# Top-32 thresholds from all 576 columns instead of folded maxima and minima, with the first attention steps ahead of the weights in the planner's order

## The chip, the cores and the metric

One core of one Trainium2 chip. The metric is the device time of one execution in microseconds (us), lower is better. Five engines work from their own instruction queues and wait for each other through semaphores: PE (TensorE, the matmuls), DVE (VectorE), ACT (ScalarE), POOL (GpSimd) and SP (SyncE, which here issues all the DMAs). Each engine takes its own instructions strictly in the order of the program.

## The reference

Sparse attention, and then two feed-forward blocks, over 4 batches of 8 heads and 576 positions of 64 (2304 tokens of 512):

```python
scores = (1 / sqrt(64)) * q @ k.T                       # [4, 8, 576, 576]
kth = np.partition(scores, -32, axis=-1)[..., -32:-31]  # the 32nd largest of each row
scores = np.where(scores >= kth, scores, -1e9)
attn = softmax(scores); x = attn @ v                    # then tokens x 512
h = x @ w_in;  g = np.maximum(0.01 * h, h);  x = g @ w_out            # 512 -> 2048 -> 512
h = np.maximum(np.maximum(x @ w1, x @ w2), x @ w3);  out = h @ w_out2 # 512 -> 768 -> 512
```

## The kernel before

**The work.** Attention is cut into 72 steps. A step takes 128 rows of queries for two heads (for the last 64 rows of a batch, four heads), and there are 18 steps to a batch. The 2304 tokens go through the feed-forward blocks in ten units of 192, 128, 256 (six times), 192 and 256 tokens. A unit has four phases on PE: H (times `w_in`), Y (times `w_out`), M (times `w1`, `w2`, `w3`) and O (times the last weight). A unit can begin when the attention steps of its tokens are done, and it is spread between later steps. Values are kept as two fp16 halves, so each product is three matmuls (`three`, lines 824 to 827).

**One step.** PE computes the scores into PSUM (L689), ACT copies them to the tile `S` (L694). DVE finds the 32nd largest score of each row: L697 folds the row of 576 into 288 maxima and 288 minima of pairs (two instructions, tile `w`), L705 (MAX8: the eight largest of a row) and L707 (MATCH_REPLACE8: overwrite these eight, with a short MATCH_VALUE_LOAD ahead of it) take turns on maxima and minima, and L711 and L715 merge the two lists. For both heads (index `j`) together that is 2 folds, 12 MAX8, 8 MATCH_REPLACE8 and the two small merges. POOL derives the softmax bias from the row's maximum (L728, tile `nb`), ACT takes the exponential (L738, tile `pp`), DVE masks (L743 for the first head, mask and product in one; L747 for the second, whose product L750 is POOL's), ACT and POOL split into halves (L752, L754, tile `phl`), a transposing DMA (L757) brings the tile `pt`, PE multiplies by V (L782 to L784, tile `av`), DVE takes the reciprocal of the row sum (L789, L791), and the block's result goes through a second transposing DMA (L819) to the tile `xu`, from which H starts.

**Weights.** They arrive as 64-bit floats. DVE rebuilds fp32 words from them (three instructions each: L479, L482, L485, 42 groups), then come norms and scales, and ACT and POOL split them into halves (L348 to L350). The 42 groups are 8 of `w_in`, 8 of `w_out`, 18 of `w1` to `w3` and 8 of the last weight. The M phase ends each tile on DVE with L966 (`k<-h,colt,k`), 12 to a unit.

**Order.** Nothing above is in program order by hand. Each instruction is first a node with an engine, an estimated duration and a priority `pr` (lower goes first); `Plan.run` plays the nodes through the five engines with these durations and writes the program in the order that comes out. So the constants `mm`, `act`, `dve`, `pool`, `dma`, the latencies and the priorities decide only the order. `TP(i)` is the priority of step `i`: 0 for the first `NE` steps and 10 + 11.9 i from then on. Weights have `wt`, which starts at 2 and grows by 1.5 to 2.1 per chunk, with extra gaps `WGT` and `WGZ` ahead of `w1` and of the last weight.

Of the kernel before, what the change touches and what calls it, by code (L numbers as in the profile page):

```python
# [12 lines left out]
I32 = mybir.dt.int32  # L13
# [6 lines left out]
HP = H // 2  # L20
# [25 lines left out]
MMO = 1.0  # L46
# [6 lines left out]
NE = 2  # L53
TE = 0.0

# [146 lines left out]
def act(n, psum=False, aps=0):  # L202
    return (n * 0.833 + (53 if psum else 93) + 93 * aps) / 1000
# [6 lines left out]
def pool(n):  # L210
    return (n * 2.08 + 60) / 1000


def dma(nbytes):
    return nbytes / 360e3
# [3 lines left out]
def attention_moe_kernel(ctx, tc, qk, v, w_in, w_out, w123, w2o, outT):  # L219
# [85 lines left out]
    def total(cols, r, pr):  # L305

        p = buf("h", [P, 512])

        def mms():
            for i, c in enumerate(cols):  # L310
                T.matmul(p()[:, :c.shape[1]], ones32, c, start=i == 0, stop=i == len(cols) - 1,
                         skip_group_check=True)

        op(PE, 0.5 * len(cols), mms, r=r, w=[p], pr=pr)
        return p

    def pow2(key, n2, n, r, pr, pre=2.0, s=None, b=None):
# [3 lines left out]
        if pre == 2.0:  # L321
            op(DVE, 0.1, lambda: V.tensor_scalar(t, (n2() if callable(n2) else n2).bitcast(I32), 24, None,
# [6 lines left out]
        op(POOL, 0.17, lambda: G.tensor_scalar(s, t, -8388608.0, 204 * 8388608.0, op0=ALU.mult, op1=ALU.add),  # L329
           r=[(key, "t")], w=[(key, "s")], pr=pr)  # L330
        op(POOL, 0.17, lambda: G.tensor_scalar(b, t, 8388608.0, 50 * 8388608.0, op0=ALU.mult, op1=ALU.add),
# [23 lines left out]
    def prep_qk(b, hp, pr, fast):  # L355
# [4 lines left out]
        for a in (1, 0):  # L360
# [20 lines left out]
        op(POOL, 0.16, lambda: G.tensor_tensor(es, bi[:, 0:1], bi[:, 1:2], op=ALU.mult),  # L381
           r=[(("qk", b, hp, a), "b") for a in range(2)], w=[(kb, 0)], pr=pr)
        op(POOL, 0.17, lambda: G.tensor_scalar(es2[:, 0:1], es, 0.125, None, op0=ALU.mult),
           r=[(kb, 0)], w=[(kb, 1)], pr=pr)
        op(POOL, 0.17, lambda: G.tensor_scalar(es2[:, 1:2], es, -0.125, None, op0=ALU.mult),
# [4 lines left out]

    DQK = {}
# [40 lines left out]
    def prep_v(b, hp, pr):  # L432
# [15 lines left out]
        op(POOL, 0.2, ones_, w=[(t, 2)], pr=pr)  # L448
# [131 lines left out]
    def fin_in(pr):  # L580
# [5 lines left out]
        op(POOL, 0.18, lambda: G.tensor_scalar(e, bin_, kap, 2.0 ** -15, op0=ALU.mult, op1=ALU.mult),  # L586
# [3 lines left out]
    def fin_out(pr):  # L590
# [14 lines left out]
        op(POOL, 0.16, lambda: G.tensor_tensor(k2, SC["kap"], SC["kap"], op=ALU.mult), r=[("kap", "s")], w=["k2"],  # L605
           pr=pr)
        op(POOL, 0.18, lambda: G.tensor_scalar(c1_, k2, s1, FCI * 2.0 ** -30, op0=ALU.mult, op1=ALU.mult),
           r=["k2", "s1"], w=["cc1"], pr=pr)
        op(POOL, 0.16, lambda: G.tensor_tensor(c2, c1_, m1, op=ALU.mult), r=["cc1", "m1"], w=["ccy"], pr=pr)
        SC["cy"] = c2  # L610

    def fin_1(pr):
# [4 lines left out]
        op(POOL, 0.18, lambda: G.tensor_scalar(e, bt, kap, 2.0 ** -15, op0=ALU.mult, op1=ALU.mult),  # L617
           r=[("kap2", "s")] + [(("w", "t", c), "b") for c in range(NF2)], w=["e_1"], pr=pr)
        op(POOL, 0.16, lambda: G.tensor_tensor(c0, ikap, SC["ikap"], op=ALU.mult),
# [3 lines left out]
    def fin_2(pr):  # L623
        b2 = col(4)
        op(POOL, 0.18, lambda: G.tensor_scalar(b2, bz, SC["c0"], 2.0 ** 30, op0=ALU.mult, op1=ALU.mult),
# [30 lines left out]
    def TP(i):  # L656
        return TE if i < NE else TA0 + TA * i

# [5 lines left out]
    def fused(i, j):  # L664
        return j < FM

    def attention(i):
# [28 lines left out]
        for x, o in ((0, ALU.max), (1, ALU.min)):  # L696
            op(DVE, dve(S), lambda x=x, o=o: V.tensor_tensor(wp()[:, :, x], Sp()[:, :, :S2], Sp()[:, :, S2:], op=o),  # L697
               r=[(Sp, 0), (Sp, 1)], w=[(wp, 0, x), (wp, 1, x)], pr=pd)
        for x, g in [(0, 0), (0, 1), (1, 0), (0, 2), (1, 1), (0, 3), (1, 2), (0, 4), (0, 5), (0, 6)]:
            for j in range(2):  # L700
                r, c0 = g // 2, TOPK * x + 8 * (g // 2)
                mc = lambda j=j, c0=c0: m()[:, j, c0:c0 + 8]
                wx = lambda j=j, x=x: wp()[:, j, x]
                if g % 2 == 0:
                    op(DVE, dve(S2), lambda mc=mc, wx=wx: V.max(mc(), wx()), r=[(wp, j, x)], w=[(m, j, x, r)], pr=pd)  # L705
                else:
                    op(DVE, dve(S2), lambda mc=mc, wx=wx: V.match_replace(  # L707
                        out=wx(), in_to_replace=mc(), in_values=wx(), imm_value=NEG),
                       r=[(m, j, x, r)], w=[(wp, j, x)], pr=pd)
        KM = TOPK // 2  # L710
        op(DVE, 0.11, lambda: V.tensor_tensor(m()[:, :, TOPK:TOPK + KM], m()[:, :, TOPK:TOPK + KM],  # L711
                                              m()[:, :, TOPK - 2:TOPK - 2 - KM:-1], op=ALU.min),
           r=[(m, j, 0, r) for j in range(2) for r in range(1, 4)], w=[(m, j, 1, r) for j in range(2) for r in range(2)],
           pr=pd)
        op(DVE, 0.11, lambda: V.tensor_reduce(m()[:, :, TOPK + KM], m()[:, :, TOPK - 1:TOPK + KM], axis=AX.X,  # L715
                                              op=ALU.max),
           r=[(m, j, 0, 3) for j in range(2)] + [(m, j, 1, r) for j in range(2) for r in range(2)],
           w=[(m, j, 2) for j in range(2)], pr=pd)
# [7 lines left out]
        if full:  # L726
            e2 = ES[b, hps[0]]
            op(POOL, 0.245, lambda: G.tensor_scalar(nb(), m()[:, :, 0:1].rearrange("p a o -> p (a o)"), e2[:, 1:2],  # L728
                                                  LNPS, op0=ALU.mult, op1=ALU.add),
# [296 lines left out]
    for hp in range(2):  # L1026
        prep_batch(0, hp)
# [111 lines left out]
```

## Time and profile before

| | |
|---|---|
| time, median of 3 runs (lowest, highest) | 1182.51 us (1181.02, 1184.38) |
| the profiled execution: its own time, its span | 1183.1 us, 1181.3 us |
| PE busy | 926.9 us (78%) |
| DVE busy | 999.3 us (85%) |
| ACT busy | 760.8 us (64%) |
| POOL busy | 755.0 us (64%) |

The span runs from the first to the last instruction of the program; the time has 1.8 us more around it. Busy time is an average over stages: attention fills the span up to 1061 us, and feed-forward work alone fills the rest.

### The profile page before, as it was taken

The numbers are of one execution on the slowest core, as the hardware profiler recorded it, in microseconds if no ns is written. First come the engines' busy times: TensorE is split into PE (matmuls) and PEld (weight loads), VectorE is DVE, ScalarE is ACT, GpSimd is POOL, SyncE is SP. The second block draws the span as 40 slices with busy tenths as digits, with TensorE's granted clock in tenths as the row PEclk, the third lists the DMA queues.
The fourth block names the chain that finished last, engine by engine and source line by source line (L and its number), as shares of the span: only waits on it lengthen the run. The fifth ranks groups of instructions, "written<-read, shape, count | busy, mean of one in ns | idle before, by whom it ended". The sixth has DMA issues, their size and how long they took to land.

```text
span 1181.3 us, 28138 instructions
## 1 busy us (share of the span) xinstructions
PE 926.9 (78%) x10294; PEld 807.8 (68%) x10294; DVE 999.3 (85%) x2970; ACT 760.8 (64%) x1625; POOL 755.0 (64%) x1054
## 2 busy tenths in 40 slices
PE   3123333568898699899899978999998998999998
PEld 2112222467788588788778867878877887799987
DVE  4869999999999989999999999999969999991001
ACT  6665766667768678666668767676676566474331
POOL 5697776677668676656767676676775566473231
PEclk9999985569899799999999999999999999999999
DMA  7786156533654635354564336525553342331000
GB/s 248 251 254 193 43 145 180 167 103 90 140 96 106 123 93 127 73 99 68 109 145 114 79 71 135 100 51 125 120 124 73 77 74 58 57 89 27 14 1 19
DMA packets 268555, 125.84 MB, mean 107 GB/s; under 512 B 237440, under 2 KB 255360, under 8 KB 266368
## 3 DMA queue, kind: packets, MB, share of 16 engines
q1 hardware_dynamic: 268416, 124.04, 44.1%
q8 instruction: 81, 1.33, 0.5%
q14 instruction: 58, 0.48, 0.1%
HBM read 62.65 MB, written 14.16 MB: 65 GB/s over the span
## 4 chain that ended last, share of the span: by engine, by line
DVE 42%; PE 22%; POOL 15%; DMA 10%; issue 6%; ACT 4%; SPq 0%; POOLq 0%; ACTq 0%; DVEq 0%
DVE m L705 14%; DVE w L707 11%; DMA pt<-phl 8%; DVE w L697 4%; PE h L826 4%; PE h L825 4%; PE h L827 4%; POOL phl L754 3%; DVE pp L743 3%; PE acc L826 2%; PE acc L827 2%; PE acc L825 2%; POOL pp L750 2%; DVE S L747 2%; PE s L689 2%
## 5 line engine op out<-in xcount | busy, mean ns | idle before, releaser
L705 DVE MAX8 m<-w 128x8 f32<-128x288 f32 x864 | 343.5, 442 | 0.0
L882 POOL TENSOR_TENSOR f16t<-k,f16t 128x256 f16<-128x256 f32 (+2 forms) x220 | 152.2, 693 | 177.7 <-ACT f16t L876 169.2
L707 DVE MATCH_REPLACE8 w<-m,w 128x288 f32<-128x288 f32 x576 | 249.3, 439 | 0.0
L754 POOL TENSOR_TENSOR phl<-pp,phl 128x576 f16<-128x576 f32 x144 | 187.4, 1310 | 32.3 <-ACT phl L752 30.3
L825 PE MATMUL h<-k,w 128*128 128x256 f16 (+2 forms) x720 | 190.2, 268 | 15.7 <-ACT k L962 9.2
L826 PE MATMUL h<-k,w 128*128 128x256 f16 (+2 forms) x720 | 190.5, 268 | 9.0 <-POOL k L924 9.0
L827 PE MATMUL h<-k,w 128*128 128x256 f16 (+2 forms) x720 | 190.6, 269 | 0.0
L826 PE MATMUL acc<-f16t,wo 128*128 128x256 f16 (+2 forms) x640 | 166.2, 264 | 8.8 <-POOL f16t L882 8.6
L825 PE MATMUL acc<-f16t,wo 128*128 128x256 f16 (+2 forms) x640 | 166.4, 264 | 0.4 <-ACT k L919 0.4
L827 PE MATMUL acc<-f16t,wo 128*128 128x256 f16 (+2 forms) x640 | 166.4, 264 | 0.0
L825 PE MATMUL h<-xu,wi 128*128 128x256 f16 (+1 forms) x576 | 156.8, 272 | 6.9 <-ACT k L869 4.6
L826 PE MATMUL h<-xu,wi 128*128 128x256 f16 (+1 forms) x576 | 156.8, 272 | 0.0
L827 PE MATMUL h<-xu,wi 128*128 128x256 f16 (+1 forms) x576 | 156.7, 272 | 0.0
L752 ACT ACTIVATE phl<-pp 128x576 f16<-128x576 f32 x144 | 97.3, 681 | 81.6 <-DVE pp L743 37.6
L750 POOL TENSOR_TENSOR pp<-pp,S 128x576 f32<-128x576 f32 x72 | 98.3, 1366 | 73.2 <-DVE S L747 53.1
L689 PE MATMUL s<-kt,qt 128*128 128x288 f16 (+5 forms) x800 | 108.5, 287 | 38.8 <-ACT S L694 37.1
L738 ACT ACTIVATE pp<-S,nb,colt 128x576 f32<-128x576 f32 x144 | 120.4, 860 | 27.7 <-POOL nb L728 17.6
L697 DVE TENSOR_TENSOR w<-S 128x576 f32<-128x576 f32 x144 | 131.0, 912 | 5.3 <-ACT S L694 5.3
L876 ACT ACTIVATE f16t<-k 128x256 f16<-128x256 f32 (+2 forms) x220 | 86.0, 391 | 61.4 <-DVE k L966 58.7
L826 PEld LDWEIGHTS <-w 128*128 128x128 f16 x960 | 95.5, 100 | 28.5 <-issue 19.7
L782 PE MATMUL av<-vt,pt 128*128 128x65 f16 (+1 forms) x800 | 90.9, 202 | 30.2 <-DMA pt<-phl 26.7
L827 PEld LDWEIGHTS <-w 128*128 128x128 f16 x960 | 95.7, 100 | 22.6 <-issue 13.9
(136 smaller groups left out, 2585.7 us busy)
## 6 DMA issues: line engine op xcount, KB each, us to landing
w<-in_w SPq DMA_DIRECT2D x18, 512.0 KB, 4.2
w<-in_w_in SPq DMA_DIRECT2D x8, 1024.0 KB, 6.0
w<-in_w_out SPq DMA_DIRECT2D x8, 1024.0 KB, 5.0
raw<-in_qk SPq DMA_DIRECT2D x24, 288.0 KB, 3.3
dqk<-hl SPq DMA_DIRECT2D x48, 144.0 KB, 2.5
kt<-dqk SPq DMA_DIRECT2D x16, 288.0 KB, 3.2
qt<-dqk SPq DMA_DIRECT2D x144, 32.0 KB, 2.3
raw<-in_v SPq DMA_DIRECT2D x12, 352.0 KB, 3.3
```

What stands on the lines that cost most here:

```text
L689: T.matmul(p()[osl, h, o:o + w], q()[:, hh, st, :n], k()[:, hh, kc:kc + w], start=st == 0, stop=st == 1, skip_group_check=True)
L697: op(DVE, dve(S), lambda x=x, o=o: V.tensor_tensor(wp()[:, :, x], Sp()[:, :, :S2], Sp()[:, :, S2:], op=o), r=[(Sp, 0), (Sp, 1)], w=[(wp, 0 ...
L705: op(DVE, dve(S2), lambda mc=mc, wx=wx: V.max(mc(), wx()), r=[(wp, j, x)], w=[(m, j, x, r)], pr=pd)
L707: op(DVE, dve(S2), lambda mc=mc, wx=wx: V.match_replace(out=wx(), in_to_replace=mc(), in_values=wx(), imm_value=NEG), r=[(m, j, x, r)], w= ...
L738: op(ACT, act(S, aps=2), lambda j=j, es=es: A.activation(pp()[:, j], Sb[j](), AF.Exp, bias=nb()[:, j:j + 1], scale=es[:, 0:1]), r=[(Sp, j) ...
L750: op(POOL, pool(S), lambda j=j: G.tensor_tensor(p2(j), p2(j), mk(j), op=ALU.mult), r=[(Sp, j)], w=[(pp, j)], pr=pr)
L752: op(ACT, act(S), lambda j=j: A.activation(phl()[:, 0, j], pp()[:, j], AF.Copy), r=[(pp, j)], w=[(phl, 0, j)], pr=pr)
L754: op(POOL, pool(S), lambda j=j: G.tensor_tensor(phl()[:, 1, j], pp()[:, j], phl()[:, 0, j], op=ALU.subtract), r=[(pp, j), (phl, 0, j)], w= ...
L825: T.matmul(out, wt(0), xt(0), start=first, stop=False, skip_group_check=True)
L826: T.matmul(out, wt(0), xt(1), start=False, stop=False, skip_group_check=True)
L827: T.matmul(out, wt(1), xt(0), start=False, stop=last, skip_group_check=True)
L882: op(POOL, pool(N) + 0.044, lambda: G.tensor_tensor(hl()[:, 1, :N], g()[:, 0, :N], hl()[:, 0, :N], op=ALU.subtract), r=[(g, 0), (hl, 0)], ...
```

## The change

The fold is left out. Each head's row of 576 scores is searched directly: four MAX8 and three MATCH_REPLACE8 over 576 columns per head, 8 and 6 per step, the first pair reading `S` itself. The threshold is the eighth value of the fourth list, so the merges are gone too. The old search stays in the code behind `fold(i)`, which gives "N" (the new search) for every step.

The planner's numbers change as well. The first four steps (`NE`) get priorities 0, 2, 4, 6 and so stand ahead of nearly all weights; the queries and keys of all four head pairs of batch 0 are prepared at the start (`range(HP)`), without the wait `GQ` for an earlier write; the gaps `WGT` and `WGZ` go to 0. Most duration estimates are raised. The planner now also lets the first unit's H phase wait for all of `w_out`, its M phase for all of `w1` to `w3` and of the last weight, and the second unit's H phase for the last weight. No instruction outside the search is added or removed.

```diff
-MMO = 1.0
+MMO = 3.0
-NE = 2
+NE = 4
 TE = 0.0
+TS = 2.0
...
-    return (n * 0.833 + (53 if psum else 93) + 93 * aps) / 1000
+    return (n * 0.833 + (70 if psum else 120) + 105 * aps) / 1000
...
-    return (n * 2.08 + 60) / 1000
+    return (n * 2.13 + 110) / 1000
...
-    return nbytes / 360e3
+    return nbytes / 255e3
...
-               r=z0 + ([("d", 0, 0, 0, 1)] if b == 0 and hp > 1 else []), pr=pr,
+               r=z0 + (GQ if b == 0 and hp > 1 else []), pr=pr,
...
+    GQ = []
...
     def TP(i):
-        return TE if i < NE else TA0 + TA * i
+        return TE + TS * i if i < NE else TA0 + TA * i
...
-        for x, o in ((0, ALU.max), (1, ALU.min)):
-            op(DVE, dve(S), lambda x=x, o=o: V.tensor_tensor(wp()[:, :, x], Sp()[:, :, :S2], Sp()[:, :, S2:], op=o),
...
+        if md == "N":
+            thr = lambda j: m()[:, j, TOPK - 1:TOPK]
+            tk = lambda j: [(m, j, 0, 3)]
+            wj = lambda j: wp()[:, j].rearrange("p x s -> p (x s)")
+            for g in range(7):
+                for j in range(2):
+                    r = g // 2
+                    mc = lambda j=j, r=r: m()[:, j, 8 * r:8 * r + 8]
+                    src = (lambda j=j: Sb[j]()) if g < 2 else (lambda j=j: wj(j))
+                    rd = [(Sp, j)] if g < 2 else [(wp, j, 0)]
+                    if g % 2 == 0:
+                        op(DVE, dve(S) * 1.03, lambda mc=mc, src=src: V.max(mc(), src()), r=rd, w=[(m, j, 0, r)], pr=pd)
+                    else:
+                        op(DVE, dve(S) * 1.03 + 0.06, lambda mc=mc, src=src, j=j: V.match_replace(
+                            out=wj(j), in_to_replace=mc(), in_values=src(), imm_value=NEG),
+                           r=[(m, j, 0, r)] + rd, w=[(wp, j, 0)], pr=pd)
...
-            wk = wkeys("i", [c])
+            wk = wkeys("i", [c]) + wkeys("o", range(8)) * (u == 0) + wkeys("z", range(4)) * (u == 1)
...
-            wk = wkeys("t", [f])
+            wk = wkeys("t", [f]) + (wkeys("t", range(NF2)) + wkeys("z", range(4))) * (u == 0)
...
-    for hp in range(2):
+    for hp in range(HP):
         prep_batch(0, hp)
...
-    WGT = 20.0
-    WGZ = 10.0
+    WGT = 0.0
+    WGZ = 0.0
...
-            ffn(nxt, t + FO * TA, between)
+            ffn(nxt, TA0 + TA * i + FO * TA, between)
```

**The search on DVE.** These are consecutive rows of DVE's order in the first step, before: the tile `S` holds the scores, `w` the folded row, `m` the lists of eight.

```order
L697 TENSOR_TENSOR w_247<-S_228 128x2x288 x2
L705 MAX m_255<-w_247 128x8 x2
L707 MATCH_REPLACE w_247<-m_255,w_247 128x288 x2
L705 MAX m_255<-w_247 128x8 x4
L707 MATCH_REPLACE w_247<-m_255,w_247 128x288 x4
L705 MAX m_255<-w_247 128x8 x4
L707 MATCH_REPLACE w_247<-m_255,w_247 128x288 x2
L705 MAX m_255<-w_247 128x8 x2
```

And of the change, the third step's search and what follows it (L722 is MAX8, L724 MATCH_REPLACE8, now on 576 columns; L484 is the first of the three instructions that rebuild a weight, here of the second group, and L326 and L433 are small scale computations):

```order
L722 MAX m_428<-S_372 128x8
L326 TENSOR_SCALAR colt<-colt 128x1
L722 MAX m_428<-S_372 128x8
L724 MATCH_REPLACE w_434<-m_428,S_372 128x576 x2
L722 MAX m_428<-w_434 128x8 x2
L724 MATCH_REPLACE w_434<-m_428,w_434 128x576 x2
L722 MAX m_428<-w_434 128x8 x2
L724 MATCH_REPLACE w_434<-m_428,w_434 128x576 x2
L722 MAX m_428<-w_434 128x8 x2
L484 TENSOR_SCALAR w_76<-w_76 128x1024
L722 MAX m_520<-S_463 128x8
```

Three whole searches now stand ahead of the second weight group on DVE; before, all 8 groups of `w_in` came between the second search and the third. Counted on DVE's order (a step is 12 MAX8 before and 8 now), the last of the 42 weight groups is rebuilt after 10.9 searches before and after 13.8 now, the first L966 of unit 0 (its M phase; L1000 in the change) stands after 12.0 and after 14.6 searches, the last one of unit 1 after 18.5 and after 21.0.

**The end of PE's order.** Before, the last product with V (tile `av`) is followed by what is left of unit 8, beginning with the last rows of its H phase (`h<-xu,wi`, 192 columns):

```order
L783 MATMUL av_16650<-vt_12664,pt_16584 64x64
L784 LDWEIGHTS pt_16584
L784 MATMUL av_16650<-vt_12664,pt_16584 64x65
L825 LDWEIGHTS wi
L825 MATMUL h_16715<-xu_14641,wi 128x192
L826 LDWEIGHTS wi
L826 MATMUL h_16715<-xu_14641,wi 128x192
```

In the change it stands in the middle of unit 8's M phase (`h<-k,w`, again 192 columns):

```order
L817 MATMUL av_16174<-vt_12597,pt_16111 64x64
L818 LDWEIGHTS pt_16111
L818 MATMUL av_16174<-vt_12597,pt_16111 64x65
L859 LDWEIGHTS w_76
L859 MATMUL h_16237<-k_2120_15907,w_76 128x192
L860 LDWEIGHTS w_76
L860 MATMUL h_16237<-k_2121_15911,w_76 128x192
```

Behind the last `av` row, PE has 336 matmuls of 192 columns and 672 of 256 before, and 156 of 192 and 672 of 256 in the change: the other 180 of unit 8 moved ahead of it.

## Rows read from the trace of the kernel before

**Rows 1.** The page: span, busy time, and the span in 40 slices (tenths busy).

```profile
span 1181.3 us, 28138 instructions
PE 926.9 (78%) x10294; PEld 807.8 (68%) x10294; DVE 999.3 (85%) x2970; ACT 760.8 (64%) x1625; POOL 755.0 (64%) x1054
...
PE   3123333568898699899899978999998998999998
...
DVE  4869999999999989999999999999969999991001
```

**Rows 2.** Windows: us, busy PE, PEld, DVE, ACT, POOL (instructions), PE clock, DMA share, GB/s.

```profile
0.00:100.00 100.00, 25.62 (x146) 17.19 (x147) 67.75 (x135) 63.98 (x109) 71.53 (x111) 1.00 0.77 243
100.00:394.00 294.00, 182.78 (x2276) 161.54 (x2275) 285.47 (x766) 203.50 (x420) 210.99 (x271) 0.83 0.50 123
394.00:1061.00 667.00, 605.58 (x6683) 525.22 (x6681) 633.95 (x2040) 452.32 (x992) 439.03 (x614) 0.97 0.45 95
1061.00:1181.30 120.30, 112.92 (x1199) 103.91 (x1195) 12.10 (x32) 41.04 (x106) 33.42 (x59) 0.99 0.06 15
...
900.00:1050.00 150.00, 141.50 (x1603) 124.00 (x1601) 146.53 (x471) 92.95 (x205) 87.49 (x117) 1.00 0.36 73
```

**Rows 3.** Timeline of DVE, the dense end of one search: start us, us, what.

```profile
671.35 1.53 DVE L705 MAX8 m<-w 128x8 f32<-128x288 f32 x4
672.80 0.07 DVE L707 MATCH_VALUE_LOAD w<-m,w 128x8 f32 x1
...
673.22 0.08 DVE L707 MATCH_VALUE_LOAD w<-m,w 128x8 f32 x1
...
677.64 0.20 DVE L711 TENSOR_TENSOR m<-m 128x32 f32<-128x32 f32 x1
677.75 0.75 DVE L697 TENSOR_TENSOR w<-S 128x576 f32<-128x576 f32 x1
678.42 0.18 DVE L715 TENSOR_REDUCE m<-m 128x2 f32<-128x34 f32 x1
```

**Rows 4.** DVE's groups by form: busy us, mean ns of one, idle before.

```profile
L697 DVE TENSOR_TENSOR w<-S 128x576 f32<-128x576 f32 x144 | 131.0, 912 | 5.3 <-ACT S L694 5.3
...
L711 DVE TENSOR_TENSOR m<-m 128x32 f32<-128x32 f32 x72 | 23.0, 320 | 1.9
```

**Rows 5.** Timeline of DVE early on: two rows back to back over 1024 columns.

```profile
47.01 1.21 DVE L482 SCALAR_TENSOR_TENSOR w<-w 128x1024 int32<-128x1024 int32 x1
48.14 1.21 DVE L482 SCALAR_TENSOR_TENSOR w<-w,w 128x1024 int32<-128x1024 int32 x1
```

**Rows 6.** Timelines of POOL and of DVE at 951 us.

```profile
951.39 0.67 POOL L882 TENSOR_TENSOR f16t<-k,f16t 128x256 f16<-128x256 f32 x1 [2.05 <-ACT f16t L876]
...
951.44 1.23 DVE L697 TENSOR_TENSOR w<-S 128x576 f32<-128x576 f32 x1
```

**Rows 7.** Timeline of DVE: the last L966 of unit 1, and the last mask.

```profile
393.44 0.34 DVE L966 SCALAR_TENSOR_TENSOR k<-h,colt,k 128x128 f32<-128x128 f32 x1
...
1060.11 0.80 DVE L747 TENSOR_SCALAR S<-S,m 128x576 f16<-128x576 f32 x1
```

**Rows 8.** Timeline of PE: the first matmul behind the last `av`.

```profile
1070.85 0.26 PE L825 MATMUL h<-xu,wi 128*128 128x192 f16 x1
```

**Rows 9.** Windows of PE alone: 192 columns; 256 columns; only `av`; only `s`; early.

```profile
1083.00:1095.00 12.00, 12.00 (x148) 1.00 0.01 2
1110.00:1140.00 30.00, 30.00 (x277) 1.00 0.01 1
...
394.00:1061.00 667.00, 65.23 (x1733) 0.97 0.45 95
...
394.00:1061.00 667.00, 69.28 (x570) 0.97 0.45 95
...
180.00:200.00 20.00, 7.40 (x86) 0.50 0.54 161
```

**Rows 10.** DVE's longest wait up to 100 us: total us, times, longest.

```profile
DVE w L479 <- POOL wi L350: 9.9, 3, 5.2
```

More of the change, by code (lines that the diff above doesn't have):

```diff
@@ L312, in mms @@
                          skip_group_check=True)
[L314 removed]
+        op(PE, 0.25 * len(cols), mms, r=r, w=[p], pr=pr)
         return p
+    SE = POOL
+    SG, SD = (G, 0.4) if SE == POOL else (V, 0.1)
     def pow2(key, n2, n, r, pr, pre=2.0, s=None, b=None):
@@ L665, in fused, with fold @@
         return j < FM
+    NBE = POOL
+    NG, ND = (G, 0.34) if NBE == POOL else (V, 0.1)
+    MODE = "N"
+    NF0 = 0
+    def fold(i):
+        return "N" if i < NF0 else MODE
     def attention(i):
@@ L710, in attention @@
-        KM = TOPK // 2
[L711 to L718, printed above, removed]
+        md = fold(i)
@@ new lines, in attention @@
+        KM = TOPK // 2
+        if md == "N":
[14 more added lines that the diff above has]
+                           r=[(m, j, 0, r)] + rd, w=[(wp, j, 0)], pr=pd)
+        else:
+            thr = lambda j: m()[:, j, TOPK + KM:]
+            tk = lambda j: [(m, j, 2)]
+            for x, o in ((0, ALU.max), (1, ALU.min)):
+                E, eng, du = (G, POOL, 1.32) if md == "P" else (V, DVE, 0.83)
+                op(eng, du, lambda x=x, o=o, E=E: E.tensor_tensor(wp()[:, :, x], Sp()[:, :, :S2], Sp()[:, :, S2:], op=o),
+                   r=[(Sp, 0), (Sp, 1)], w=[(wp, 0, x), (wp, 1, x)], pr=pd)
+            for x, g in [(0, 0), (0, 1), (1, 0), (0, 2), (1, 1), (0, 3), (1, 2), (0, 4), (0, 5), (0, 6)]:
+                for j in range(2):
+                    r, c0 = g // 2, TOPK * x + 8 * (g // 2)
+                    mc = lambda j=j, c0=c0: m()[:, j, c0:c0 + 8]
+                    wx = lambda j=j, x=x: wp()[:, j, x]
+                    if g % 2 == 0:
+                        op(DVE, 0.375, lambda mc=mc, wx=wx: V.max(mc(), wx()), r=[(wp, j, x)], w=[(m, j, x, r)], pr=pd)
+                    else:
+                        op(DVE, 0.427, lambda mc=mc, wx=wx: V.match_replace(
+                            out=wx(), in_to_replace=mc(), in_values=wx(), imm_value=NEG),
+                           r=[(m, j, x, r)], w=[(wp, j, x)], pr=pd)
+            op(DVE, 0.2, lambda: V.tensor_tensor(m()[:, :, TOPK:TOPK + KM], m()[:, :, TOPK:TOPK + KM],
+                                                 m()[:, :, TOPK - 2:TOPK - 2 - KM:-1], op=ALU.min),
+               r=[(m, j, 0, r) for j in range(2) for r in range(1, 4)], w=[(m, j, 1, r) for j in range(2) for r in range(2)],
+               pr=pd)
+            op(DVE, 0.2, lambda: V.tensor_reduce(m()[:, :, TOPK + KM], m()[:, :, TOPK - 1:TOPK + KM], axis=AX.X,
+                                                 op=ALU.max),
+               r=[(m, j, 0, 3) for j in range(2)] + [(m, j, 1, r) for j in range(2) for r in range(2)],
+               w=[(m, j, 2) for j in range(2)], pr=pd)
@@ L930, in ffn @@
            r=[(yh, e) for e in range(4)], w=[(ff2[0], 0), (ff2[0], 1), ("yn", u)], pr=pr)
-        op(PE, 0.5, lambda: T.matmul(acc(0)[:, :1], part32, n2, start=True, stop=True, skip_group_check=True),
+        op(PE, 0.25, lambda: T.matmul(acc(0)[:, :1], part32, n2, start=True, stop=True, skip_group_check=True),
            r=[("yn", u)], w=[ak(0)], pr=pr)
@@ L1060, in attention_moe_kernel @@
     seen = set()
-    for hp in range(2):
+    for hp in range(HP):
         seen.add((0, hp))
```

70 lines of the change are left out of this document (29 added, 41 removed).

## The prediction

> **What bounds the kernel now.** I read the page's slices first [rows 1]: DVE stands at nine tenths from the fourth slice to about 1060 us and at zero to one after it, while PE only then never stops. So there are two stages. The windows say by how much [rows 2]. From 100 to 1061 us DVE is busy 919.4 of 961 us: it sets the pace. PE is busy 605.6 of 667 us between 394 and 1061 us, a share of 0.908, close enough to become the limit itself. From 1061 us to the end PE works off a backlog (112.9 of 120.3 us) and DVE has almost nothing to do. In the first 100 us DVE is idle for 32 us. A gain must therefore come from less DVE work per step, from a smaller backlog of PE when attention ends, or from the first 100 us.
>
> **The search.** It goes from 22 large instructions a step to 14 longer ones. Dense prices, from one start to the next [rows 3]: four MAX8 from 671.35 to 672.80 us, 0.362 each; a MATCH_REPLACE8 with its load 0.42, from 672.80 to 673.22; a fold 0.67, from 677.75 to 678.42; the merge L711 0.11. A fold is rarely that cheap: its mean duration is 912 ns [rows 4] against the 750 of the dense one [rows 3], so I add 0.16 and get 0.83. L711 is 320 ns in the mean against 200, which makes 0.23, and L715 costs about 0.1. In front of L711 DVE waits 0.12 for the last MAX8, which either search does at its end. The old search: 12 x 0.362 + 8 x 0.42 + 2 x 0.83 + 0.23 + 0.1 + 0.12 = 9.81 us.
>
> The new instructions are not in the trace: MAX8 and MATCH_REPLACE8 over 576 columns. What 288 more columns cost is taken from other rows. A DVE instruction over 1024 fp32 columns takes 1.13 from start to start [rows 5], one over 576 columns 0.67 [rows 3]: 0.46 us for 448 columns, 1.03 ns a column, so 288 columns add 0.296. The new search: 8 x 0.658 + 6 x 0.716 + 0.12 = 9.68 us. That saves 0.13 a step; I take 0.1, because a short wait may stand between dependent instructions, and 72 steps give **-7 us**. The bounds: if twice the columns cost twice the time, 8 x 0.724 + 6 x 0.84 + 0.12 = 10.95, 1.14 more a step and +82 us; if the folds' extra time stayed somewhere in the step, the saving would turn into +0.2 a step, +14 us; if the waits vanish too, -0.2 a step, -14 us. I stay near the low end, since the rows with twice the columns show no second pass.
>
> What the folds' extra time is can be seen at 951 us [rows 6]: the fold that meets a POOL instruction of 0.67 us takes 1.23 in place of 0.75, as if it had stood still for most of it. The Trainium skill (SBUF — State Buffer, "SBUF: two separate sides") has the rule for it: a VectorE instruction with two SBUF inputs and a GpSimd instruction exclude each other for the whole of the one that came first. By that rule the 0.16 goes with the folds, since MAX8 reads one tensor, and the term is the -7 above; by the bound without it, +14. The trace agrees with the rule at this place.
>
> Edits that cost nothing: the maximum for the softmax bias is ready earlier, but POOL and ACT are busy only 439 and 452 of 667 us [rows 2] and wait behind DVE; the mask reads another column of the same tile; the PE, ACT, POOL and DMA instructions are the same in number. If the exponential did come late, DVE's mask would wait for it, within the two or three steps that the three buffers of `S` allow.
>
> **The first 100 us.** Steps 0 to 3 now stand ahead of the weights. DVE idles 32 us there [rows 2], 9.9 of them because POOL had not yet split a weight and freed its buffer [rows 10]; searches need nothing from POOL, so they can fill this hole. I take half of it, **-5 us**; the bounds are -10 and +10, the latter if the scale computations of all four head pairs, which now stand ahead of the first search in DVE's order, come late (SP's queue has eight loads of queries and keys ahead of it, where four stood before).
>
> **The end.** Behind the last `av`, PE has 180 matmuls of 192 columns fewer. 148 of them take 12.0 us [rows 9], 81 ns each: **-14.6 us**. Before, 336 x 0.081 + 672 x 0.108 (30 us for 277 [rows 9]) is 99.8 us, out of the 110.5 from 1070.85 [rows 8] to the end; 10.7 us are waits and the output. Now it is 85.2, and with the same 10.7 the end comes 95.9 us after the last `av`. The transposing DMA to `xu` must land before the last unit's H phase; before, 5.6 us passed between the last `av` and its first matmul, and 156 x 0.081 = 12.6 us of unit 8 cover that now.
>
> **What it costs to get there.** The matmuls that left the end must be done earlier, and unit 1's last L966 stands 2.5 searches later in DVE's order, since M of unit 0 waits for all weights. In the trace that L966 is at 394 us and the last mask ends at 1061 [rows 7], the last `av` at 1071. A step costs DVE more than its search, 9.8 us, and less than 634 us by 53.5 steps, 11.9 [rows 2], which holds the feed-forward rows too; I take 11.2, so 2.5 steps are 28 us. DVE's clock: 394 + 28 - 2 (the search of 21 steps) - 5 = 415 us for unit 1, and 677 - 28 - 5 = 644 us from there to the last `av`. PE's clock: it was busy 606 us in the old stretch, and about 9 of the 10 us behind it. Take away 2.5 steps of attention, 134.5 us for 53.5 steps [rows 9], so 6 us, and add 14.6: 624 us of work in 644. That is a share of 0.968, where it had 0.908, and 0.943 at its best stretch of any length, 900 to 1050 us [rows 2], in which DVE still set the pace (146.5 of 150). I take 0.955, between that and what is asked: 624 / 0.955 = 653, **+9 us** over DVE's clock. The bounds are 0 (PE follows) and +42 (0.908 again).
>
> **The sum**, against the profiled execution's own 1183.1 us (1181.3 of span and 1.8 around it; the median of the runs shown is 1182.5, the same within what a measurement can tell, 0.3% or 3.5 us): 1183.1 - 7 - 5 - 14.6 + 9 = 1165.5, so **1166 us**.
>
> **The rivals.**
> - *PE keeps pace.* No wait is added, and the early hole is filled whole: 1183.1 - 7 - 10 - 14.6 = 1152. For it: much of PE's idle time in the stretch is there because DVE paces it. Against: 0.968 is more than any stretch with attention shows.
> - *PE does not keep pace* (the other side: slower). If its share stays 0.908, 624 / 0.908 = 687 us, the last `av` comes at 415 + 687 = 1102, the end 95.9 later at 1198, the time is 1200. It decides from a share of 624 / (1181.3 - 95.9 - 415) = 0.931 downwards, which lies between the two shares that the trace shows. Then DVE waits inside the stretch for L1000's inputs and for `av`.
> - *Unit 0 runs at the low clock.* M of unit 0 now stands 2.6 searches later, behind a gap of some 28 us in which PE has only attention, 2.5 us a step. In 180 to 200 us PE was busy 7.4 us of 20 and the granted clock was 0.50, the 1.2 GHz level [rows 9]. If the clock is at that level when M starts, its 216 matmuls take twice 17.5 us; the sum with it is 1166 + 17 = 1183, no change. The Trainium skill (TensorE: Matmul & The Clock Gate, "HAM oscillation — how this bites in real kernels") says that idle gaps of PE put the clock back to the low level. No run here shows yet what this gap does; the price and the chance are from the rows.
> - *Twice the columns cost twice the time.* Then DVE alone adds 82 us and PE has slack again: 1183 + 82 - 5 - 15 = 1245.
>
> **How the numbers follow.** Forecast 0.42 (faster by 1.4%), PE keeps pace 0.18 (faster), low clock or mixtures that cancel 0.18 (same), PE does not keep pace 0.17 and the doubled search 0.05 (slower). So faster 0.60, same 0.18, slower 0.22. The range reaches from 1140, ten below the better rival for more early gain, to 1195, just under the full price of the slower one; outside lie the doubled search and the worst of PE's share. The forecast's own range is 1156 to 1176.
>
> **What would show it.** MAX8 over 576 columns from start to start: 0.66 us says right, 0.72 or more wrong. The search per step in a dense stretch: 9.7. DVE idle up to 100 us: 27. The last L1000 of unit 1: 415 us. PE's share from there to the last `av`: 0.95 or more; DVE's waits for PE there grow from almost nothing if it is lower. From the last `av` to the end: 96 us. The granted clock when unit 0's M starts. I am wrong if the last `av` does not come before 1075 us, whatever the search costs.

## The result and the profile after

The change takes 1166.55 us (median of 4 runs, 1165.0 to 1167.53) where the kernel before takes 1182.78 us (4 runs, 1181.02 to 1184.38): a ratio of 0.9842, with a 95% interval from 0.9809 to 0.9875. It is faster by 1.6%; 1166 had been forecast. Of the kernels below, one execution (both engines lighter, 1409 us at a granted clock of 0.671) ran in a slower state and is left out of its median.

The page of the change first: span, busy times, the slices of PE and DVE, and the chain that ended last (the other rows of before are in [rows 1]). The last line is the chain of before.

```profile
span 1163.2 us, 27290 instructions
PE 923.0 (79%) x10294; PEld 807.4 (69%) x10294; DVE 998.8 (86%) x2106; ACT 758.5 (65%) x1625; POOL 728.9 (63%) x1054
...
PE   3252234675389899789899978998999999999998
...
DVE  3999999999999999899996999989989999994001
...
PE 51%; DVE 20%; POOL 8%; ACT 7%; DMA 7%; issue 4%; SPq 1%; POOLq 0%; ACTq 0%; DVEq 0%
```

```profile
DVE 42%; PE 22%; POOL 15%; DMA 10%; issue 6%; ACT 4%; SPq 0%; POOLq 0%; ACTq 0%; DVEq 0%
```

DVE has 864 instructions fewer and is busy for the same time as before, 998.8 us against 999.3. The chain, which ran over DVE, now runs over PE. The time went elsewhere, and windows between the three events that the prediction named show where: the end of unit 1's last L1000 (393.8 us before, 412.6 now) and the end of the last `av` (1070.9 and 1069.5). First the last two windows of before, cut at these events, then the four of the change. The columns are those of [rows 2].

```profile
394.00:1070.90 676.90, 615.48 (x6859) 534.88 (x6857) 634.27 (x2042) 456.49 (x1005) 445.52 (x622) 0.97 0.44 95
1070.90:1181.30 110.40, 103.02 (x1019) 94.25 (x1018) 11.77 (x30) 36.87 (x93) 26.93 (x51) 0.99 0.04 11
```

```profile
0.00:100.00 100.00, 36.28 (x260) 23.96 (x261) 79.11 (x149) 69.02 (x124) 65.57 (x110) 0.82 0.72 220
100.00:412.60 312.60, 182.30 (x2278) 162.44 (x2278) 302.46 (x593) 209.71 (x430) 219.87 (x288) 0.72 0.51 130
412.60:1069.50 656.90, 616.68 (x6922) 541.80 (x6922) 608.08 (x1344) 448.89 (x998) 422.05 (x620) 0.98 0.42 94
1069.50:1163.20 93.70, 87.72 (x836) 79.20 (x835) 9.11 (x23) 30.86 (x75) 21.46 (x38) 1.00 0.04 13
```

Read as three pieces, the span lost 18.1 us: +18.8 up to unit 1's end, -20.2 in the long stretch, -16.7 behind the last `av`. The same sum read on PE: it is busy 3.9 us less, and idle 14 us less. Idle time up to unit 1's end went from 186 to 194 us, in the long stretch from 61 to 40, behind it from 7 to 6. In the long stretch PE does the same work, 616.7 us against 615.5, in 20 us less. (Idle time is a window's length less the busy time in its row.) So the gain is that PE waits less between 412 and 1070 us. DVE idles more there than before, 49 us against 43.

These rows of the change mark the events (DVE's timeline, then PE's; 1054.23 is the last mask, 1069.40 the first matmul behind the last `av`):

```profile
412.23 0.34 DVE L1000 SCALAR_TENSOR_TENSOR k<-h,colt,k 128x128 f32<-128x128 f32 x1
...
1054.23 0.81 DVE L781 TENSOR_SCALAR S<-S,m 128x576 f16<-128x576 f32 x1
...
1069.40 0.26 PE L859 MATMUL h<-k,w 128*128 128x192 f16 x1
```

The search itself, in a dense piece of DVE's timeline of the change:

```profile
675.74 1.41 DVE L722 MAX8 m<-w 128x8 f32<-128x576 f32 x2
677.07 0.07 DVE L724 MATCH_VALUE_LOAD w<-m,w 128x8 f32 x1
677.13 0.74 DVE L724 MATCH_REPLACE8 w<-m,w 128x576 f32<-128x576 f32 x1
677.78 0.08 DVE L724 MATCH_VALUE_LOAD w<-m,w 128x8 f32 x1
677.85 0.74 DVE L724 MATCH_REPLACE8 w<-m,w 128x576 f32<-128x576 f32 x1
678.51 1.41 DVE L722 MAX8 m<-w 128x8 f32<-128x576 f32 x2
```

Two MAX8 over 576 columns take 1.33 us from start to start, 0.665 each; a MATCH_REPLACE8 with its load takes 0.71 and 0.73. Added up over the trace, from each search instruction's start to the next instruction's start (or to its own end, if DVE idles behind it), all 72 searches take 710.1 us before and 702.2 now.

The weights' rebuilding took that gain back. Its instructions are the same, and their busy time rose from 126.1 to 135.8 us. These are its three lines, over the whole span, first of before and then of the change (the third column is DVE's busy time in them):

```profile
0.00:1181.30 1181.30, 33.77 (x42) 0.94 0.45 107
0.00:1181.30 1181.30, 44.53 (x42) 0.94 0.45 107
0.00:1181.30 1181.30, 47.82 (x42) 0.94 0.45 107
...
0.00:1163.20 1163.20, 35.80 (x42) 0.90 0.44 108
0.00:1163.20 1163.20, 46.18 (x42) 0.90 0.44 108
0.00:1163.20 1163.20, 53.80 (x42) 0.90 0.44 108
```

In the change they stand between searches, and POOL works beside 108 us of them, where it was beside 93. The timeline at one place, rows of DVE and POOL, shows what that does:

```profile
118.76 1.21 DVE L490 SCALAR_TENSOR_TENSOR w<-w,w 128x1024 int32<-128x1024 int32 x1
118.85 1.16 POOL L333 TENSOR_SCALAR colt<-colt 128x1 int32<-128x1 int32 x1 [2.17 <-DVE colt L587]
...
123.26 0.19 POOL L333 TENSOR_SCALAR colt<-colt 128x1 int32<-128x1 int32 x1
...
128.35 2.11 POOL L354 TENSOR_TENSOR wo<-w,wo 128x1024 f16<-128x1024 f32 x1
...
128.37 3.17 DVE L490 SCALAR_TENSOR_TENSOR w<-w,w 128x1024 int32<-128x1024 int32 x1
```

The same two-input instruction takes 1.21 us where it starts first, and 3.17 where a POOL instruction started 0.02 us ahead of it: POOL's 2.09 that are left, and then 1.1 of its own. Where DVE starts first, POOL stands still: its one-column instruction takes 1.16 us there and 0.19 at 123.26. This is the rule that the prediction named for the folds (the Trainium skill, SBUF — State Buffer, "SBUF: two separate sides"). The trace agrees with it here.

That the weights lose more time is a matter of the order, and not of the folds' absence. The same three lines, in the kernel with the old search and the new order, and in the one with the new search and the old planner (both below), add up to 140.7 and 127.6 us:

```profile
0.00:1175.00 1175.00, 38.10 (x42) 0.94 0.44 107
0.00:1175.00 1175.00, 51.96 (x42) 0.94 0.44 107
0.00:1175.00 1175.00, 50.63 (x42) 0.94 0.44 107
...
0.00:1194.20 1194.20, 33.37 (x42) 0.93 0.45 105
0.00:1194.20 1194.20, 48.73 (x42) 0.93 0.45 105
0.00:1194.20 1194.20, 45.53 (x42) 0.93 0.45 105
```

### The profile page after: what moved, and what is told of

It is laid out like the page before. It is cut to its first block, busy times and chain, and to the rows that moved or that the text cites. A ratio compares the mean times of both kernels' runs of the same rounds, so it can differ in the third digit from the quotient of the medians.

```text
span 1163.2 us, 27290 instructions
## 1 busy us (share of the span) xinstructions
PE 923.0 (79%) x10294; PEld 807.4 (69%) x10294; DVE 998.8 (86%) x2106; ACT 758.5 (65%) x1625; POOL 728.9 (63%) x1054
## 3 DMA queue, kind: packets, MB, share of 16 engines
q8 instruction: 81, 1.33, 0.5%
## 4 chain that ended last, share of the span: by engine, by line
PE 51%; DVE 20%; POOL 8%; ACT 7%; DMA 7%; issue 4%; SPq 1%; POOLq 0%; ACTq 0%; DVEq 0%
PE h L859 9%; PE h L860 9%; PE h L861 9%; DMA pt<-phl 6%; PE acc L860 5%; PE acc L861 5%; PE acc L859 5%; DVE m L722 5%; DVE w L724 4%; PE s L702 3%; DVE w L487 3%; DVE w L490 2%; POOL phl L788 2%; PE av L816 2%; DVE w L484 2%
## 5 line engine op out<-in xcount | busy, mean ns | idle before, releaser
L722 DVE MAX8 m<-w 128x8 f32<-128x576 f32 x432 | 310.2, 747 | 0.3
L916 POOL TENSOR_TENSOR f16t<-k,f16t 128x256 f16<-128x256 f32 (+2 forms) x220 | 143.4, 654 | 183.6 <-ACT f16t L910 174.9
L788 POOL TENSOR_TENSOR phl<-pp,phl 128x576 f16<-128x576 f32 x144 | 189.8, 1325 | 36.3 <-ACT phl L786 35.2
L724 DVE MATCH_REPLACE8 w<-m,w 128x576 f32<-128x576 f32 x288 | 212.1, 741 | 0.0
L784 POOL TENSOR_TENSOR pp<-pp,S 128x576 f32<-128x576 f32 x72 | 93.7, 1301 | 58.3 <-DVE S L781 34.8
L860 PEld LDWEIGHTS <-w 128*128 128x128 f16 x960 | 95.3, 99 | 36.8 <-issue 27.9
L702 PEld LDWEIGHTS <-qt 128*128 128x128 f16 (+1 forms) x800 | 64.5, 109 | 79.4 <-issue 54.9
L903 ACT ACTIVATE k<-h,colt 128x256 f32<-128x256 f32 (+2 forms) x160 | 71.3, 449 | 69.9 <-PE h L861 67.8
L707 ACT ACTIVATE S<-s 128x576 f32<-128x576 f32 x144 | 92.7, 644 | 36.0 <-PE s L702 30.0
```

The lines of the kernel that those rows point to most:

```text
L702: T.matmul(p()[osl, h, o:o + w], q()[:, hh, st, :n], k()[:, hh, kc:kc + w], start=st == 0, stop=st == 1, skip_group_check=True)
L707: op(ACT, act(S, True), lambda t=t, p=p: A.activation(t().rearrange("p (a s) -> p a s", a=2), p()[:, :, :288], AF.Copy), r=[p], w=[(Sp, j) ...
L722: op(DVE, dve(S) * 1.03, lambda mc=mc, src=src: V.max(mc(), src()), r=rd, w=[(m, j, 0, r)], pr=pd)
L724: op(DVE, dve(S) * 1.03 + 0.06, lambda mc=mc, src=src, j=j: V.match_replace(out=wj(j), in_to_replace=mc(), in_values=src(), imm_value=NEG) ...
L784: op(POOL, pool(S), lambda j=j: G.tensor_tensor(p2(j), p2(j), mk(j), op=ALU.mult), r=[(Sp, j)], w=[(pp, j)], pr=pr)
L788: op(POOL, pool(S), lambda j=j: G.tensor_tensor(phl()[:, 1, j], pp()[:, j], phl()[:, 0, j], op=ALU.subtract), r=[(pp, j), (phl, 0, j)], w= ...
```

## The experiments

All differ from the change unless it says otherwise. The table gives each one's time, its ratio to the kernel before in the same series of runs, and the three pieces of its profiled execution: end of unit 1's last L1000 (L966 in the kernel before), the stretch from there to the last `av`, the rest of the span, and PE's share of the stretch. The three pieces add up to the span of that execution, which with its 1.8 us was 2 to 4 us quicker than the median for the kernels with two first steps and with the old durations, and 5 us slower for the new search in the old order. Wherever an edit changes what the planner reads, it writes another order; only in the kernels with one engine or both lighter (but not "made anew") and in the one with DVE heavier is the order that of the change.

| kernel | median us | ratio (95%) | unit 1 | stretch | rest | PE share |
|---|---|---|---|---|---|---|
| before | 1182.78 | | 393.8 | 677.1 | 110.4 | 0.909 |
| the change | 1166.55 | 0.984 (0.981 to 0.988) | 412.6 | 656.9 | 93.7 | 0.939 |
| old search, new order | 1175.29 | 0.992 (0.989 to 0.994) | 411.9 | 673.1 | 90.0 | 0.932 |
| new search, old order | 1190.95 | 1.007 (1.004 to 1.010) | 394.5 | 710.4 | 89.3 | 0.901 |
| two first steps | 1175.87 | 0.993 (0.990 to 0.996) | 408.9 | 673.1 | 89.8 | 0.925 |
| M of unit 0 free | 1168.26 | 0.985 (0.980 to 0.990) | 389.0 | 684.7 | 93.7 | 0.916 |
| PE lighter | 1157.22 | 0.977 (0.973 to 0.980) | 411.9 | 652.3 | 90.7 | 0.884 |
| DVE lighter | 1168.54 | 0.986 (0.983 to 0.990) | 412.7 | 659.2 | 93.7 | 0.935 |
| both lighter | 1155.92 | 0.977 (0.975 to 0.978) | 411.5 | 651.9 | 90.7 | 0.887 |
| both lighter, order made anew | 1092.91 | 0.923 (0.920 to 0.926) | 413.9 | 563.5 | 114.2 | 0.952 |
| DVE heavier | 1177.75 | 0.996 (0.994 to 0.997) | 414.6 | 667.2 | 93.7 | 0.927 |
| old durations | 1180.08 | 0.997 (0.995 to 1.000) | 402.0 | 684.6 | 88.4 | 0.925 |
| order moved a little | 1165.31 | 0.985 (0.984 to 0.987) | 413.7 | 656.1 | 93.7 | 0.933 |
| old priorities, new durations | 1194.52 | 1.009 (1.006 to 1.011) | 424.1 | 663.7 | 104.6 | 0.916 |

**The search and the order, apart.** First the old, folded search in the planner of the change (the edit below); then the new search in the kernel before, whose planner stays as it was.

```diff
-    MODE = "N"
+    MODE = "V"
```

> The old folded search, all else as in the change, the planner's new numbers included; in the order that results, unit 1's last L1000 stands after 19.8 searches (21.0 in the change) and PE has 111 matmuls of 192 columns behind the last av (156). My sum by terms: the search gives back its 8 us, the end is 45 x 0.081 = 4 us shorter, so 1171, and the change's time is split between search and order. Rival, the order does it all and the search nothing: 1163. Rival, the search is what counts (it also took POOL's contention away): 1180 or more.

> The new search in the kernel before, with the planner's old numbers and the old order of the first steps; unit 1's last feed-forward instruction on DVE stands after 18.2 searches, and 102 matmuls of 192 columns are left behind the last av, since the planner counts 10.0 us for the new search and 8.9 for the old. By my terms: -7 for the search, -19 for the end, no early gain, and PE must be busy 0.945 of the stretch to the last av, so about 1162. Rival, the first steps ahead of the weights carry the gain: 1176 or more.

The first came at 1175, four above what was expected: the new planner keeps about half of the gain without the new search. The second missed by 29 us, and on the other side: with the new search alone the old kernel is slower. Its long stretch, and the longest wait of its PE for a transfer, with that of the kernel before behind it (microseconds in all, times, longest):

```profile
394.50:1104.90 710.40, 639.90 (x7099) 554.36 (x7099) 639.13 (x1414) 466.90 (x1030) 433.06 (x639) 0.97 0.44 91
```

```profile
PE av L774 <- DMA pt<-phl: 39.6, 29, 5.0
...
PE av L782 <- DMA pt<-phl: 26.7, 20, 7.4
```

More of PE's work came ahead of the last `av` (639.9 us, where before had 615.5), which shortened the end by 21 us. But PE's idle time in the stretch rose from 61 to 70 us, and its waits for `pt` in the whole run from 26.7 to 39.6. So the new search is worth -9 us with the planner's new numbers and +8 with the old ones. The order moved with the search in both pairs, so neither shows the search alone. A saving on DVE is not paid out as such.

**The four first steps.** The two constants go back to those of before:

```diff
-NE = 4
+NE = 2
-TS = 2.0
+TS = 0.0
```

> The change with only the first two steps ahead of the weights (NE 2, TS 0, as before). By my terms the early gain of 5 to 10 us is lost and the end is 48 x 0.081 = 4 us shorter: 1168 to 1173, and DVE's idle time up to 100 us is back near 30. Rival, what DVE does not do early it does later without loss, since PE sets the end: 1163.

DVE idles 19.6 us of the first 100, not the 30 that would have shown that these two constants fill the early hole (the change has 20.9, before 32.3 [rows 2]). The kernel is 9 us slower all the same, 3 above the range that was expected, and the profiled execution loses 16 us in the long stretch, 673 against 657, of which it gets 8 back outside it. The gain of this edit is real; that it lies in the early hole is not so.

**Unit 0's M without its wait for all weights.**

```diff
-            wk = wkeys("t", [f]) + (wkeys("t", range(NF2)) + wkeys("z", range(4))) * (u == 0)
+            wk = wkeys("t", [f])
```

> The change without the planner's rule that unit 0's M phase waits for all of w1 to w3 and the last weight; its first L1000 stands after 11.9 searches (14.6), unit 1's last after 18.8 (21.0), 156 matmuls behind the last av as in the change. If PE's pace costs 9 us or more in the long stretch, 2.2 steps more time for the same matmuls give it back: 1157 or less, and the granted clock has no second low stretch before M. Rival, the late M costs nothing because DVE sets the pace: 1166.

Unit 1 ends 23.6 us sooner, and the time is that of the change: the stretch behind it grows by 27.8, with 10.8 more of PE's work in it and 17 us more of idle time. That M starts late costs nothing that these runs can tell; they are wide apart here, 1159.4 to 1170.4 us.

**PE lighter, DVE lighter.** Two experiments with the change's order kept to the instruction. One leaves out a third of M in units 2 to 8, the other the last round of each search from step 21 on. Of long lines only the part that changes is shown.

```diff
-    def three(out, wt, xt, first, last):
+    def three(out, wt, xt, first, last, full=True):
-        T.matmul(out, wt(0), xt(1), start=False, stop=False, skip_group_check=True)
+        full and T.matmul(out, wt(0), xt(1), start=False, stop=False, skip_group_check=True)
...
-                        k == 0, k == KC - 1), r=[(yh, k), (yl, k)] + wk, w=[p], pr=pr)
+                        k == 0, k == KC - 1, not 2 <= u <= 8), r=[(yh, k), (yl, k)] + wk, w=[p], pr=pr)
```

> Same order on every engine; of the three matmuls per product the second is left out in the M phase of units 2 to 8 (504 matmuls: 72 of 256 columns in each of six units, 72 of 192 in one; unit 9, which makes the end, keeps all), so the output differs. That takes 53 us from PE and nothing from DVE, nearly all before the last av. If PE's pace costs 9 us over DVE's clock, as I said: 1153 to 1158. Rival, PE is the limit of the long stretch: 1115 to 1125. Rival, DVE alone is: 1164 to 1166.

```diff
-            thr = lambda j: m()[:, j, TOPK - 1:TOPK]
+            thr = lambda j: m()[:, j, 23:24] if i >= 21 else m()[:, j, TOPK - 1:TOPK]
...
-lambda mc=mc, src=src: V.max(mc(), src())
+lambda mc=mc, src=src, g=g: None if i >= 21 and g > 4 else V.max(mc(), src())
```

(and the same condition ahead of `V.match_replace`.)

> Same order on every engine; the last MATCH_REPLACE8 and the last MAX8 of each head are left out from step 21 on (four DVE instructions a step, 51 steps; the threshold is the 24th largest there, so the output differs). That takes 51 x 2.8 = 143 us from DVE and nothing from PE. If PE's own 617 us then set the stretch of 657 us: 30 to 40 us less, 1127 to 1137. Rival, DVE is the only limit: 1025 to 1050. Rival, PE is the limit already: 1155 or more.

The long stretch of each, PE lighter first, and DVE's longest wait of the second (20.8 us, 28 times, in the change):

```profile
411.90:1064.20 652.30, 576.76 (x6454) 495.80 (x6454) 605.64 (x1345) 447.61 (x998) 420.34 (x620) 0.98 0.44 95
```

```profile
412.70:1071.90 659.20, 616.22 (x6921) 540.38 (x6921) 472.52 (x1038) 447.50 (x998) 424.16 (x620) 0.98 0.42 94
```

```profile
DVE r L823 <- PE av L818: 81.1, 43, 4.5
```

DVE has 136 us less to do in the stretch, and the stretch is no shorter (659 against 657 us): it waits for `av` instead. Whatever set the pace, it was not DVE's work. PE is busy 40 us less in its stretch, which is 4.6 us shorter (652.3 against 656.9); another 3.0 come off behind the last `av`, where a part of unit 8's M stands. The median is 9 us lower. Neither engine's work is the limit by itself.

**Both lighter, in the old order and in a new one.** The first has both edits above. The second tells the planner too, with a duration of 0.001 for what is left out on DVE and `t3 * 2 / 3` for the lighter M.

> Both lightenings together, in the order of the change: one of three matmuls left out in M of units 2 to 8 (504 matmuls, about 53 us of PE) and the last MATCH_REPLACE8 and MAX8 of each head left out from step 21 (about 143 us of DVE); the output is not the reference's. Alone the first gave 9 us and the second nothing. Theory (PE and DVE are limits side by side, and nothing else is): with DVE out of the way PE's 53 us count in full at a share of about 0.94, so the last av comes about 55 us sooner and the time is 1103 to 1115. Rival (a chain over ACT, POOL and DMA, or the order itself, is a third limit close behind): 1140 to 1157, hardly better than the first alone. If 1120 to 1135, part of each.

> The same work left out as in the run of both lightenings (a third of M of units 2 to 8 on PE, the last round of each search on DVE from step 21; the output is not the reference's), but the planner is told so, and writes a new order for it. By that order 387 matmuls of 192 columns and 672 of 256 stand behind the last av. If the fixed order is the third limit that held the run of both lightenings at 1156 (each engine waits in order for results that were planned for later), the new one lets the last av come 60 us or more sooner and the time is 1105 to 1130. If a chain of fixed length over ACT, POOL and the DMAs to pt is that limit, whatever the order, the time stays at 1145 to 1157.

Their long stretches, old order first:

```profile
411.50:1063.40 651.90, 577.95 (x6454) 497.06 (x6454) 471.30 (x1038) 447.24 (x998) 420.93 (x620) 0.98 0.44 95
```

```profile
413.90:977.40 563.50, 536.66 (x6184) 473.45 (x6184) 465.21 (x1031) 437.15 (x970) 413.96 (x602) 0.99 0.50 110
```

With both engines lighter at once the time is that of PE lighter alone, 1156: PE idles 74 us of its stretch and DVE 181. The same instructions in an order that knows of it take 1093, 12 below the lower end that was expected, and PE idles 27 us of a shorter stretch (0.952). Part of the shorter stretch is work put off: PE has 107 us behind the last `av`, where it had 85. Over the whole span PE idles 46 us less, out of 62.5 that the span lost. So for this lighter work a third limit exists, and it is the order. I read it so: the program fixes which row of which step or unit stands next on each engine; where the planned times and the true ones part, the engines wait for each other in turn, and work taken from one is handed back as a wait for another. A chain of fixed length over ACT, POOL and the transfers would have held the second kernel too. It did not.

**DVE heavier.** One more MAX8 per step from step 21, into columns that nothing reads:

```diff
-lambda mc=mc, src=src: V.max(mc(), src())
+lambda mc=mc, src=src, g=g, j=j: (V.max(mc(), src()), i >= 21 and g == 4 and j == 0 and V.max(m()[:, 0, 32:40], src()))
```

> One more MAX8 over 576 columns per step from step 21 (0.67 us for 51 steps, 34 us of DVE); its result goes to columns that nothing reads, the order is that of the change. If DVE is a limit right behind PE, the last mask and the last av move by most of it: 1190 to 1200. If DVE has slack that the wait for PE now leaves, 10 to 17 us at most: 1167 to 1180. DVE idles some 45 us of the stretch of 657 us (share 0.93), so nothing at all is not expected.

It costs 11 us for 34 (51 times 0.665; DVE's busy time on the page is 26.8 more): DVE idles 32 us of the stretch instead of 49, and PE 48 instead of 40. Work added to DVE is paid for by a third of it or somewhat more, work taken away is worth nothing.

**Which part of the planner's numbers.** The change with the four estimates of before (`MMO`, `act`, `pool`, `dma`, as in the change's diff), then the control with one estimate moved by 2%, then the kernel before with the new search, the four new estimates and the waits `wkeys` of the first two units. That last one keeps all else of before: `NE`, the gaps, the loads at the start, and the smaller single durations that the change also raised.

> The change with the planner's duration estimates of before (MMO, act, pool, dma) and all its other edits: the order alone differs. By the order, only 21 matmuls of 192 columns are left behind the last av (156 in the change), unit 1's last L1000 stands 1.25 searches sooner. If the priorities made the gain, 1160 to 1170. If the calibrated durations made it, because an order played with true durations has fewer waits of the engines for each other, 1180 or more, and PE's share of the long stretch at 0.91.

> A control: the change with one duration estimate moved by 2% (DMA bytes per us 250e3 in place of 255e3), which means nothing by itself and gives another order of the same instructions. If a difference of 8 us between two kernels with different orders has a cause of its own, this one comes at 1163 to 1171. If an order's details alone are worth as much, 1175 or more, or 1158 or less, and then the single order edits are not to be read one by one.

> The order of before (its NE, TA, gaps and early loads) with three things of the change: the new search, the four raised duration estimates, and the waits of the first two units for the later weights, without which no order comes out. Against the run of the new search alone (1191) and that of the change with the old estimates (1180). If the estimates make the gain, 1163 to 1172. If the priorities are as much needed, 1175 to 1185; by the order there is more left behind the last av (285 matmuls of 192 columns, 156 in the change), so the last av would have to come some 10 us sooner than the change's for the same time.

The old estimates cost 13.5 of the 16 us, although less is left behind the last `av` (88.4 us against 93.7): PE idles 51 us of the stretch. The control, whose order is another one (the last weight group is rebuilt after 14.1 searches, not 13.8), comes at 1165, within what a measurement can tell of the change. So I read the differences of 8 us and more as more than the luck of an order, on the word of this one control. The last one was expected at 1163 to 1172 if the estimates sufficed and at 1175 to 1185 if the priorities were needed too; it came at 1194.5, above both. It is later at each event: unit 1 by 11.5 us, the stretch by 6.8, the rest by 10.9. These four estimates without the rest of the new planner are worth nothing either; which part of that rest is needed, the priorities or the single durations, no run tells apart.

## Why the prediction was right, and where its reasons were not

The three events came where they were put. Unit 1 ended at 412.6 us (415 forecast), the stretch took 656.9 (653), the rest 93.7 (95.9): 1163.2 in all where 1163.9 was forecast, and 1.8 around it. These come from counted positions in the orders and from durations of the trace, and they held. That the total is right to half a microsecond is luck: the three pieces are off by -2.4, +3.9 and -2.2. By its steps:

- **The search, -7**: right as a price. MAX8 0.665 us (0.658 forecast), MATCH_REPLACE8 with its load 0.72 (0.716), all searches -7.9 us. The doubled price (+82) is out. "The folds' extra time" left with the folds, as forecast. But DVE's whole busy time stayed (999.3 and 998.8 us), because the new order cost the rebuilding of weights 9.7 us, which the prediction had not looked at.
- **The first 100 us, -5**: DVE idles 20.9 us there, 11 less than before [rows 2] and more than the 5 forecast. The reason given, that the first steps fill the hole, did not hold: with two first steps it is filled too.
- **The end, -14.6**: -16.7. The counted matmuls carry it; PE's idle time behind the last `av` fell by another 1.4.
- **PE's pace, +9**: 0.939 where 0.955 was forecast, so 657 us instead of 653, and 13 over the "DVE's clock" of 644. Two misses nearly cancel here. At the lower share 624 us of work would have taken 664 and not 653; but PE had 616.7 us of work in the stretch, which takes 8 back: 10.4 us of work and not 6 had moved ahead of unit 1's end (PE is busy 218.6 us up to there, before 208.2), and PE's whole busy time fell by 3.9. The share was between the two that had been named, 0.908 and 0.968, and above the 0.931 from which the change would have been slower.

**The step that failed** is the first: "it sets the pace", said of DVE, and with it the search's 7 us in the sum of "DVE's clock". DVE was at 0.94 of the stretch, and I took a high share for the limit. In the change's order 136 us less of DVE's work changed nothing (1168.5), and the same saving of the search came with +8 us under the old planner. The stretch got shorter because the new priorities and the new estimates together let PE wait 21 us less: it needs both (1180 without the four estimates, 1194.5 with them and the rest of the old planner, 1191 with neither). My +9 for PE was a loss on a clock that did not run; the right size came from the bounds by PE's share. That the new search is worth 9 us under the new planner (1175 without it) is measured, and its reason is not shown. The size fits the price that the heavier DVE showed: with the folds DVE is busy 1019.0 us, 20 more than in the change, since masks and weights lose time too, and 11 us for 26.8 of busy time would make that 8.

**The rivals.** "PE keeps pace" (1152) did not come: 0.968 of the long stretch is more than any of these kernels with the full work shows. (That no stretch of before showed as much was read wrongly: from 895 to 945 us PE was busy 48.9 of 50 us. It is the long stretches that stay below.) "PE does not keep pace" did not come either, but its mechanism is what the kernel with the new search alone shows (0.901, 1191). "Unit 0 runs at the low clock" had the gap right and the price wrong. The windows of the change around the start of M, and four rows of PE in it:

```profile
270.00:300.00 30.00, 11.51 (x86) 9.00 (x86) 29.00 (x59) 20.52 (x47) 24.00 (x35) 0.60 0.43 110
300.00:330.00 30.00, 13.50 (x137) 10.57 (x137) 27.23 (x64) 17.32 (x37) 17.10 (x20) 0.56 0.52 130
330.00:360.00 30.00, 30.00 (x419) 29.57 (x418) 27.93 (x65) 19.42 (x45) 13.79 (x22) 0.99 0.61 129
```

```profile
326.88 0.36 PE L859 MATMUL h<-k,w 128*128 128x192 f16 x1
327.04 0.36 PE L860 MATMUL h<-k,w 128*128 128x192 f16 x1
...
330.51 0.25 PE L861 MATMUL h<-k,w 128*128 128x192 f16 x1
330.59 0.25 PE L859 MATMUL h<-k,w 128*128 128x192 f16 x1
```

The granted clock was at 0.56 to 0.60 before M, with PE busy 11.5 and 13.5 of 30 us. M starts at 326.88 with matmuls 0.16 us apart, twice the 0.081 of the full clock, and from 330.51 on they are at the full clock. The slow piece is 3.6 us long and costs under 2 us, not 17. What the prediction cited on idle gaps (the Trainium skill, TensorE: Matmul & The Clock Gate, "HAM oscillation — how this bites in real kernels") agrees with the trace for the gap (0.56 to 0.60). The forecast of this rival went wrong behind it: the clock was back 3.6 us after the dense matmuls began, and the rival had all 216 of them at the low level. Over the whole program the four runs of the change had granted clocks of 0.899, 0.948, 0.904 and 0.905, and their times lie within 2.6 us.

**What stays open.** Which wait of the fixed order binds is not settled. In the kernel with both engines lighter PE waits 24 us for `pt` between 420 and 1060 us and DVE 87 for `av`, which are two sides of the same loop (scores, search, mask, halves, `pt`, `av`). No run took one link of it away. Nor was a version found that beats the change with the full work, so that the order also holds the full work back is argued from the lighter one and not shown. And one control, with one estimate moved, is all that speaks for what an order's details are worth.

## What to carry to other kernels

A busy share of 0.94 does not name the limit of a kernel whose engines take their work in a planned order: the work of an engine is the limit only if taking it away shortens the time, and here 136 us less on the busiest engine did nothing (34 us more cost 11). Where a planner writes the order, its durations and priorities can be worth as much as the instructions. Here they had to be set together, and to be played again after a change of work: the same lighter work took 1156 us in the old order and 1093 in its own. The same saving that came with a gain under the new planner came with a loss under the old one (1191).

## What was not expected of the hardware

The contention of DVE and POOL was expected of the folds alone, and it was larger elsewhere: a two-input DVE instruction over 1024 columns took 1.21 us where it started first and 3.17 where POOL's of 2.11 us had started just ahead, and the rebuilding of weights took from 126.1 to 140.7 us by the order it stood in. The other price was forecast, and the trace now shows it: MAX8 and MATCH_REPLACE8 over twice the columns took less than twice as long, 0.665 us against 0.362 [rows 3] and 0.72 against 0.42, so that 14 long instructions cost no more than 22 shorter ones.
